# Attention and token mixing in one kernel: the two heads of a pair normalised together, the first batches' scale by another engine, and a new order

## The chip, the cores and the metric

The kernel runs on one core of a Trainium2 chip. The metric is the device time of one execution in microseconds; the median of several executions counts. An execution is a little longer than the span, which goes from the first to the last instruction of the profile. Engines by their names in the profile: PE is TensorE (PEld its weight loads), DVE VectorE, ACT ScalarE, POOL GpSimd, SP the queue that issues the DMAs.

## The reference

```python
# q, k, v: [8, 8, 576, 64] fp32 (batch, head, position, dim)
scores = scale * q @ k.T - slope[h] * |rel|,  masked to 0 <= rel < 128
attn = softmax(scores)                      # + 1e-9 in the denominator
x = (attn @ v), heads side by side          # [8, 576, 512]
theta = x @ w_theta
zr, zi = x * cos(theta), x * sin(theta)
y = w_tok_r @ zr + w_tok_i @ zi             # over positions
u = x + y
out = u + relu(u @ w_ch)
```

q and k are scaled up by about 6.7 before the kernel sees them. All inputs are fp32.

## The kernel before

The kernel writes its steps into a `Plan`: each step has an engine, a cost, the buffers that it reads and writes, and a function that emits its instructions. `Plan.order` simulates the steps by their costs, sorts them by due times, shifts these by the random draws of the seeds in `NUDGES`, and `Plan.run` emits the steps in the order that comes out. So the order on every queue is fixed by the costs, the dependencies and the seeds. Where the plan leaves TensorE idle, `spin` (L363) puts filler matmuls of `white`, into the free columns of the banks of the attention outputs (L367).

Work goes batch by batch, 32 pairs of heads in all, four pairs to a batch. `scores` (L608) does a pair: TensorE's products into `s_ps` (L621), VectorE's bias and minimum (L631), ScalarE's exponential (L635). The first seven pairs (`EARLY`) are transposed on TensorE (L677), copied by ScalarE (L679) and multiplied with v in fp32 (L687). For later pairs the weights are split in two fp16 halves (L644, L646), transposed by a DMA (L649) and multiplied with v split likewise (L601, L603, L705). Head 2p writes into bank `a_psa`, head 2p+1 into `a_psb`. `finish` (L655) then does three VectorE steps for each head: the denominator (L660), its reciprocal (L663) and the normalisation of 320 columns into `x_sb` (L664).

When a batch's eight heads stand, `turn` makes theta and z: x split and transposed by DMA (L811, L812, L816; for batch 0 also by TensorE, L826), theta (L757), range reduction and sine and cosine (L771 to L781), the product with x (L785), z in two fp16 halves (L790, and L411 for the lower half, by VectorE for batches under `QUICK` and by GpSimd for the others). `mix` (L862) and `channels` (L890) are TensorE's large products for the batch before; L868, L872, L875 and L898, L901, L905 are their elementwise steps.

`measure(b)` (L503) finds a power of two by which batch b's v is scaled. For batches under `SUMMED` ScalarE sums |v| over a group of four heads (L516, twice a batch), and VectorE and TensorE turn the sums into one scale (L525 to L545). For the others VectorE takes each head's largest |v| (L521, twice a batch), and L548 to L561 make the scale. What follows (L565 to L568) is common. An early head's `finish` needs that scale's inverse.

The weights come as fp32 and are unpacked on the chip ahead of batch 0's `mix`: `unpack` (L413) loads a chunk (L422) and takes its magnitude (L426 on ScalarE), its low bits (L436 on ScalarE for the first `LOW_C` chunks of `wch`, L440 on VectorE for the others) and puts them together (L432, L443, L452). `halve` splits them in fp16 halves (L478, L481).

Of the kernel before, what the change touches and what calls it, by code (L numbers as in the profile page):

```python
# [25 lines left out]
NT = 5  # L26
# [8 lines left out]
EARLY = 7  # L35
QUICK = 2
# [3 lines left out]
SUMMED = 2  # L40
# [6 lines left out]
LOW_C = 1  # L47
# [5 lines left out]
while RAD * 0.5 > math.pi:  # L53
# [240 lines left out]
def attn_moe_kernel(ctx: ExitStack, tc: tile.TileContext, qt, kt, vx, wth, wtok, wch, band, out):  # L294
# [30 lines left out]
    mx_ring, den_ring = small(2 * NT, 4), small(NT, 4)  # L325
# [35 lines left out]
    a_ring, t_ring, m_ring = banks("a_ps", 2), banks("t_ps", 2), banks("m_ps", 2)  # L361
# [51 lines left out]
    def unpack(src, c, w, held, last, first, summed, magnitude, lowest, raw_buf=None):  # L413
# [8 lines left out]
        issued.append(plan("SP", (0.42, w * 2.55e-3, 2.15), lambda: nc.sync.dma_start(  # L422
# [80 lines left out]
    def measure(b):  # L503
# [6 lines left out]
        for k in range(2):  # L510
            vb = group_v[2 * b + k]
            part = most.tile[:, GROUP * k:GROUP * k + GROUP]
            if b < SUMMED:
# [10 lines left out]
        if b < SUMMED:  # L524
# [71 lines left out]
    def split_values(n):  # L596
        vb, k, (scale, rise, _) = group_v[n // GROUP], n % GROUP, group_scale[n // H]
        buf = v_ring.take()
        vh, vl = buf.tile
        v, vs = vb.tile[:, k, :, :64], scale.tile[:, n % H:n % H + 1]  # L600
        plan("ACT", (0.508, 0.15), lambda: nc.scalar.activation(vh[:, :, :64], v, AF.Copy, scale=vs),  # L601
             r=[(vb, 0), (scale, 0)], w=[(buf, "h")])
        plan("DVE", (0.53, 0.13), lambda: nc.vector.scalar_tensor_tensor(  # L603
            out=vl, in0=v, scalar=vs, in1=vh[:, :, :64], op0=ALU.mult, op1=ALU.subtract),
            r=[(vb, 0), (scale, 0), (buf, "h")], w=[(buf, "l")], port=True)
        return buf, rise.tile[:, n % H:n % H + 1], rise
# [48 lines left out]
    def finish(n, acc, x_buf, vs, read, tiny):  # L655
        h = n % H
        av = acc.tile[:, :NT * 65].rearrange("p (i d) -> p i d", d=65)
        den_buf = den_ring.take()
        den = den_buf.tile[:, :, None]
        plan("DVE", (0.134, 0.13), lambda: nc.vector.tensor_scalar(  # L660
            out=den, in0=av[:, :, 64:65], scalar1=tiny, scalar2=vs, op0=ALU.add, op1=ALU.mult), r=[(acc, 0)] + read,
            w=[(den_buf, 0)])
        plan("DVE", (0.075, 0.13), lambda: nc.vector.reciprocal(out=den, in_=den), w=[(den_buf, 0)])  # L663
        plan("DVE", dve(320), lambda: nc.vector.tensor_tensor(  # L664
            out=x_buf.tile[:, :, h * D:(h + 1) * D], in0=av[:, :, :64], in1=den.broadcast_to([128, NT, D]),
            op=ALU.mult), r=[(acc, 0), (den_buf, 0)], w=[(x_buf, h)])

    def early_head(n, weights, x_buf):
# [22 lines left out]
        finish(n, acc, x_buf, zs.tile[:, 1:2], [(zs, 1)], 1.0e-9)  # L691

    def late_head(n, weights, x_buf):
# [15 lines left out]
        finish(n, acc, x_buf, vs, [(scale, 0)], 1.0e-9 * 2.0 ** PEXP)  # L709
# [259 lines left out]
    for b in range(B):  # L969
        x_buf = x_ring.take()  # L970
        for g in range(PAIRS_OF):
# [5 lines left out]
            for e in range(2):  # L977
                head = early_head if p < EARLY else late_head
                head(2 * p + e, pair_weights[p][e], x_buf)
# [61 lines left out]
```

## Time and profile before

| | |
|---|---|
| median of the runs | 609.73 us (608.84 to 610.28, 3 runs) |
| the profiled execution | 614.84 us |
| its span | 613.0 us |
| instructions in the span | 14313 |

How to read the rows further down: a group of instructions is given by its line, engine and operation, the tile written and the tiles read, the shape, the count, then the busy time in us and the mean of one in ns, then the idle time of the engine just ahead of them with what ended it. A timeline row has the start, the duration, the engine, the line, the tile written and read, and in brackets the idle time ahead of it and its releaser. Neighbours on one engine overlap in these rows, so what an instruction costs a full engine is the distance from its start to the next one's. In a view of the chain, each piece has its start and its length. The granted clock of TensorE is a share of full speed.

### The profile page before, as it was taken

The numbers are of one execution on the slowest core, as the hardware profiler recorded it, in microseconds if no ns is written. First come the engines' busy times: TensorE is split into PE (matmuls) and PEld (weight loads), VectorE is DVE, ScalarE is ACT, GpSimd is POOL, SyncE is SP. The second block draws the span as 40 slices with busy tenths as digits, with TensorE's granted clock in tenths as the row PEclk, the third lists the DMA queues.
The fourth block names the chain that finished last, engine by engine and source line by source line (L and its number), as shares of the span: only waits on it lengthen the run. The fifth ranks groups of instructions, "written<-read, shape, count | busy, mean of one in ns | idle before, by whom it ended". The sixth has DMA issues, their size and how long they took to land.

```text
span 613.0 us, 14313 instructions
## 1 busy us (share of the span) xinstructions
PE 596.3 (97%) x5417; PEld 438.9 (72%) x5417; DVE 531.4 (87%) x1568; ACT 498.8 (81%) x923; POOL 150.4 (25%) x133
## 2 busy tenths in 40 slices
PE   8997999999998999999999999999999999999997
PEld 6786756886676766776677767777677668776775
DVE  5798999999998999899898999999989999658433
ACT  4998999968998889996999689978899699246312
POOL 1000120011240215621474114231232133415100
PEclk9899999999998999999999999999999999999999
DMA  8784762399559892897569775989156734211102
GB/s 313 295 287 148 186 152 57 90 214 183 109 149 218 143 164 68 201 202 165 86 156 226 153 129 120 239 125 209 58 137 143 132 51 108 74 36 39 49 1 78
DMA packets 165541, 87.24 MB, mean 142 GB/s; under 512 B 144736, under 2 KB 153056, under 8 KB 165472
## 3 DMA queue, kind: packets, MB, share of 16 engines
q1 hardware_dynamic: 165472, 86.33, 61.1%
q8 instruction: 42, 0.69, 0.5%
q14 instruction: 27, 0.22, 0.1%
HBM read 41.22 MB, written 9.44 MB: 83 GB/s over the span
## 4 chain that ended last, share of the span: by engine, by line
PE 66%; ACT 18%; DMA 6%; DVE 6%; issue 2%; SPq 1%; POOL 0%; ACTq 0%; DVEq 0%
PE m_psb L862 15%; PE m_psa L862 15%; PE s_ps L621 7%; PE m_psa L890 7%; PE m_psb L890 6%; PE t_psa L757 5%; PE t_psb L757 5%; PE a_psb L705 3%; PE a_psa L705 3%; DMA ptd<-hlb 2%; DMA vbb<-in_vx_dram 2%; ACT sbb L635 2%; ACT sba L635 1%; ACT sbc L635 1%; ACT z_hi L790 1%
## 5 line engine op out<-in xcount | busy, mean ns | idle before, releaser
L862 PEld LDWEIGHTS <-z_hi 128*128 128x128 f16 x1152 | 110.2, 98 | 35.9 <-issue 6.3
L890 PEld LDWEIGHTS <-wch 128*128 128x128 f16 x768 | 73.8, 98 | 24.2 <-issue 4.4
L862 PE MATMUL m_psb<-wtk_hi,z_hi 128*128 128x288 f16 x288 | 82.9, 288 | 0.0
L862 PE MATMUL m_psb<-wtk_hi,z_lo 128*128 128x288 f16 x288 | 82.9, 288 | 0.0
L862 PE MATMUL m_psb<-wtk_lo,z_hi 128*128 128x288 f16 x288 | 82.9, 288 | 0.0
L862 PE MATMUL m_psa<-wtk_hi,z_hi 128*128 128x288 f16 x288 | 82.7, 287 | 0.0
L862 PE MATMUL m_psa<-wtk_lo,z_hi 128*128 128x288 f16 x288 | 82.5, 286 | 0.0
L862 PE MATMUL m_psa<-wtk_hi,z_lo 128*128 128x288 f16 x288 | 82.4, 286 | 0.0
L862 PEld LDWEIGHTS <-z_lo 128*128 128x128 f16 x576 | 56.5, 98 | 14.8 <-DVE z_lo L411 0.3
L411 POOL TENSOR_TENSOR z_lo<-wch_held,z_hi 128x512 f16<-128x512 f32 x28 | 36.8, 1329 | 67.8 <-ACT z_hi L790 67.7
L890 PE MATMUL m_psa<-u,wch 128*128 128x288 f16 x384 | 52.3, 286 | 0.8 <-ACT u_spare L898 0.8
L890 PE MATMUL m_psb<-u,wch 128*128 128x288 f16 x384 | 52.3, 286 | 0.0
L635 ACT ACTIVATE sba<-sba,fixed 128x256 f32<-128x256 f32 (+2 forms) x110 | 44.8, 460 | 3.0 <-DVE fixed L631 2.7
L812 POOL TENSOR_TENSOR hlxa<-x_sba,hlxa 128x512 f16<-128x512 f32 (+1 forms) x12 | 15.4, 1279 | 126.4 <-ACT hlxa L811 126.3
L635 ACT ACTIVATE sbc<-sbc,fixed 128x256 f32<-128x256 f32 (+2 forms) x106 | 43.3, 459 | 3.0 <-DVE fixed L631 2.9
L635 ACT ACTIVATE sbb<-sbb,fixed 128x256 f32<-128x256 f32 (+2 forms) x104 | 42.6, 462 | 3.7 <-DVE fixed L631 3.7
L757 PEld LDWEIGHTS <-xpa 128*128 128x128 f16 x224 | 21.5, 98 | 23.9 <-issue 0.7
L631 DVE CUSTOM_DVE_ANT_0 sba<-s_ps,bands 128x256 f32<-128x256 f32 (+2 forms) x110 | 35.4, 357 | 3.5 <-PE s_ps L621 3.4
L757 PEld LDWEIGHTS <-xpb 128*128 128x128 f16 x224 | 21.3, 98 | 23.5 <-issue 0.7
L631 DVE CUSTOM_DVE_ANT_0 sbc<-s_ps,bands 128x256 f32<-128x256 f32 (+2 forms) x106 | 33.7, 356 | 3.2 <-PE s_ps L621 3.1
L872 ACT ACTIVATE u<-xtfb,fixed 128x288 f16<-128x288 f32 x32 | 16.6, 526 | 24.1 <-DVE xtfb L868 24.1
L631 DVE CUSTOM_DVE_ANT_0 sbb<-s_ps,bands 128x256 f32<-128x256 f32 (+2 forms) x104 | 33.6, 358 | 1.7 <-PE s_ps L621 1.7
(325 smaller groups left out, 1576.9 us busy)
## 6 DMA issues: line engine op xcount, KB each, us to landing
vba<-in_vx_dram SPq DMA_DIRECT2D x6, 780.0 KB, 5.5
out_dram<-xtfa SPq DMA_DIRECT2D x32, 144.0 KB, 2.0
out_dram<-xtfb SPq DMA_DIRECT2D x32, 144.0 KB, 1.8
vbb<-in_vx_dram SPq DMA_DIRECT2D x5, 780.0 KB, 5.6
vbc<-in_vx_dram SPq DMA_DIRECT2D x5, 780.0 KB, 5.6
kra<-in_kt_dram SPq DMA_DIRECT2D x11, 288.0 KB, 4.6
qra<-in_qt_dram SPq DMA_DIRECT2D x11, 288.0 KB, 4.3
qrb<-in_qt_dram SPq DMA_DIRECT2D x11, 288.0 KB, 3.4
```

What stands on the lines that cost most here:

```text
L411: plan(engine, cost, lambda: on.tensor_tensor(out=out, in0=whole, in1=part, op=ALU.subtract), r=r, w=w, port=True)
L621: nc.tensor.matmul(ps.tile[:qn, e, at:at + kn], qr.tile[rows, q0:q0 + qn], kr.tile[rows, k0:k0 + kn], start=True, stop=True)
L631: kn=kn, c0=c0: nc.vector.tensor_tensor_reduce(out=part, in0=source, in1=bands[:qn, (2 * p + e) % H, c0:c0 + kn], scale=-0.125, scalar=3.0 ...
L635: plan("ACT", (0.187 + kn * 0.833e-3, 0.15), lambda part=part, least=least: nc.scalar.activation(part, part, AF.Exp, bias=least, scale=-1. ...
L705: nc.tensor.matmul(av[:, to[0]:to[1], :d], l, r, start=n in STARTS and j == 0, stop=n in STOPS and j == 2)
L757: nc.tensor.matmul(t_ps, a[:, c * 128:c * 128 + 128], w[:, c, :], start=(k == 0 and c == 0), stop=(k == len(prods) - 1 and c == 3))
L790: plan("ACT", (0.52, 0.15), lambda: nc.scalar.copy(z_hi[:, c, :], z), r=key, w=[(z_buf, ("h", c))])
L812: plan("POOL", pool(512), lambda: nc.gpsimd.tensor_tensor(out=lo, in0=x, in1=hi, op=ALU.subtract), r=every + [(hlx, "h")], w=[(hlx, "l")])
L862: nc.tensor.matmul(y.tile[:, :HALF], z[:, c, m * 128:m * 128 + 128], w[:, c, cs], start=(part == 0 and j == 0 and a == 0), stop=(part == 2 ...
L872: plan("ACT", (0.43, 0.15), lambda m=m, cs=cs, at=at: nc.scalar.activation(u_hi[:, m, cs], at, AF.Copy, scale=share), r=[(xtf, ("y", m, hf ...
L890: nc.tensor.matmul(o.tile[:, :HALF], w[:, c, e * 128:e * 128 + 128], u[:, c, cs], start=(k == 0), stop=(k == 11))
```

## The change

The two banks become one tile of two banks, and both heads of a pair end in one `finish`: one denominator step and one reciprocal step over ten columns, then two normalisations as before, one for each head. All of them come behind the second head's product. The ring of denominators holds three pairs where it held four heads.

`SUMMED` is empty: the first two batches' scale comes from VectorE's maximum (L521) like the others'. `QUICK` goes from 2 to 1: the lower half of batch 1's z is made by GpSimd. `LOW_C` goes from 1 to 0: the low bits of the first chunk of `wch` are taken by VectorE. The planned time of the first three weight loads is 0.7 us longer. The seeds are others, and with the costs they give another order of all steps.

```diff
--- before.py
+++ after.py
@@ -33,18 +33,18 @@
 PAIRS = B * H // 2
 PAIRS_OF = H // 2
 EARLY = 7
-QUICK = 2
+QUICK = 1
 TURNED = 0
 TRUE = 3
 MIXED = 1
-SUMMED = 2
+SUMMED = ()
 LIFT = 2.0 ** 16
 ABS_T = 4
 ABS_W = 9
 ABS_C = 4
 LOW_T = 4
 LOW_W = 5
-LOW_C = 1
+LOW_C = 0
 VALUES = ((0, 0), (1, 2))
 
 MAGIC = 1.5 * 2.0 ** 23
@@ -76,12 +76,12 @@
 ROUNDS = 6
 SELF = {"DVE": 0.115, "ACT": 0.13, "POOL": 0.1}
 NUDGES = (
...
 )
 
 
@@ -322,7 +322,7 @@
         assert columns_at[0] <= 320
         return Ring([fixed[:, at + k * width:at + (k + 1) * width] for k in range(count)])
 
-    mx_ring, den_ring = small(2 * NT, 4), small(NT, 4)
+    mx_ring, den_ring = small(2 * NT, 4), small(2 * NT, 3)
     most_ring, whole_ring, spread_ring, scale_ring, rise_ring = (small(H, n) for n in (1, 1, 1, 2, 2))
     zs_ring = small(8, 3)
     white, pale = place("white", [128, 256], BF16), place("pale", [128, 128], BF16)
@@ -358,7 +358,8 @@
     xp_ring = ring("xp", 2, [128, 2, 512], F16)
 
     s_ring = Ring([psum.tile([128, 2, 512], F32, name="s_ps")])
-    a_ring, t_ring, m_ring = banks("a_ps", 2), banks("t_ps", 2), banks("m_ps", 2)
+    pairs_ps = psum.tile([128, 2, 512], F32, name="a_ps")
+    a_ring, t_ring, m_ring = Ring([pairs_ps[:, e] for e in range(2)]), banks("t_ps", 2), banks("m_ps", 2)
 
     def spin(tile, count):
 
@@ -419,7 +420,8 @@
         R, E, M = ((raw_buf, k) for k in "rem")
         ex, low = t[:, 2 * S:2 * S + w], t[:, 3 * S:3 * S + w]
         powers = ex.bitcast(BF16).rearrange("p (n t) -> p n t", t=2)[:, :, 1]
-        issued.append(plan("SP", (0.42, w * 2.55e-3, 2.15), lambda: nc.sync.dma_start(
+        issued.append(plan("SP", (0.42, w * 2.55e-3 + (0.7 if len(issued) < 3 else 0.0), 2.15),
+                           lambda: nc.sync.dma_start(
             out=t[:, :2 * w], in_=src[:, c, :].bitcast(I32)), w=[R]))
         plan.follow(issued[-1], begin)
         if magnitude:
@@ -510,7 +512,7 @@
         for k in range(2):
             vb = group_v[2 * b + k]
             part = most.tile[:, GROUP * k:GROUP * k + GROUP]
-            if b < SUMMED:
+            if b in SUMMED:
                 spare = hl_ring.tiles[k].bitcast(BF16).rearrange("p a b c -> p (a b c)")[:, :GROUP * NT * 64].rearrange(
                     "p (h c d) -> p h c d", h=GROUP, d=64)
                 taken = plan("ACT", (1.26, 0.15), lambda vb=vb, spare=spare, k=k: nc.scalar.activation(
@@ -521,7 +523,7 @@
                 plan("DVE", (1.395, 0.13), lambda vb=vb, part=part: nc.vector.tensor_reduce(
                     out=part, in_=vb.tile[:, :, 1:, :64], axis=mybir.AxisListType.XY, op=ALU.max,
                     apply_absolute_value=True), r=[(vb, 0)], w=[(most, k)])
-        if b < SUMMED:
+        if b in SUMMED:
             plan("DVE", (0.075, 0.13), lambda: nc.vector.tensor_tensor(
                 out=most.tile.rearrange("p (k h) -> p k h", h=GROUP),
                 in0=spread.tile[:, :2, None].broadcast_to([128, 2, GROUP]),
@@ -603,7 +605,8 @@
         plan("DVE", (0.53, 0.13), lambda: nc.vector.scalar_tensor_tensor(
             out=vl, in0=v, scalar=vs, in1=vh[:, :, :64], op0=ALU.mult, op1=ALU.subtract),
             r=[(vb, 0), (scale, 0), (buf, "h")], w=[(buf, "l")], port=True)
-        return buf, rise.tile[:, n % H:n % H + 1], rise
+        first = n % H // 2 * 2
+        return buf, rise.tile[:, first:first + 2, None].broadcast_to([128, 2, NT]), rise
 
     def scores(p, weights):
         late = p >= EARLY
@@ -652,20 +655,24 @@
             for e in range(2):
                 weights[e][group] = pt, ptv[:, e]
 
-    def finish(n, acc, x_buf, vs, read, tiny):
-        h = n % H
-        av = acc.tile[:, :NT * 65].rearrange("p (i d) -> p i d", d=65)
+    def finish(p, accs, x_buf, vs, read, tiny):
+
+        h = 2 * p % H
+        av = pairs_ps[:, :, :NT * 65].rearrange("p e (i d) -> p e i d", d=65)
         den_buf = den_ring.take()
-        den = den_buf.tile[:, :, None]
-        plan("DVE", (0.134, 0.13), lambda: nc.vector.tensor_scalar(
-            out=den, in0=av[:, :, 64:65], scalar1=tiny, scalar2=vs, op0=ALU.add, op1=ALU.mult), r=[(acc, 0)] + read,
+        den = den_buf.tile.rearrange("p (e i) -> p e i", e=2)
+        banks = [(acc, 0) for acc in accs]
+        plan("DVE", (0.15, 0.13), lambda: nc.vector.scalar_tensor_tensor(
+            out=den, in0=av[:, :, :, 64], scalar=tiny, in1=vs, op0=ALU.add, op1=ALU.mult), r=banks + read,
             w=[(den_buf, 0)])
-        plan("DVE", (0.075, 0.13), lambda: nc.vector.reciprocal(out=den, in_=den), w=[(den_buf, 0)])
-        plan("DVE", dve(320), lambda: nc.vector.tensor_tensor(
-            out=x_buf.tile[:, :, h * D:(h + 1) * D], in0=av[:, :, :64], in1=den.broadcast_to([128, NT, D]),
-            op=ALU.mult), r=[(acc, 0), (den_buf, 0)], w=[(x_buf, h)])
-
-    def early_head(n, weights, x_buf):
+        plan("DVE", (0.08, 0.13), lambda: nc.vector.reciprocal(out=den, in_=den), w=[(den_buf, 0)])
+        for e in range(2):
+            plan("DVE", dve(320), lambda e=e: nc.vector.tensor_tensor(
+                out=x_buf.tile[:, :, (h + e) * D:(h + e + 1) * D], in0=av[:, e, :, :64],
+                in1=den[:, e, :, None].broadcast_to([128, NT, D]), op=ALU.mult), r=[(accs[e], 0), (den_buf, 0)],
+                w=[(x_buf, h + e)])
+
+    def early_head(n, weights):
         vb, k = group_v[n // GROUP], n % GROUP
         pt = pt_ring.take()
         for group in range(2):
@@ -688,9 +695,9 @@
                                  start=n in STARTS, stop=n in STOPS)
         plan("PE", pe(1840), multiply, r=[(pt, 0), (pt, 1), (vb, 0)], w=[(acc, 0)])
         zs = group_scale[n // H][2]
-        finish(n, acc, x_buf, zs.tile[:, 1:2], [(zs, 1)], 1.0e-9)
-
-    def late_head(n, weights, x_buf):
+        return acc, zs.tile[:, 1:2, None].broadcast_to([128, 2, NT]), [(zs, 1)], 1.0e-9
+
+    def late_head(n, weights):
         buf, vs, scale = split_values(n)
         acc = a_ring.take()
         av = acc.tile[:, :NT * 65].rearrange("p (i d) -> p i d", d=65)
@@ -706,7 +713,7 @@
                                      stop=n in STOPS and j == 2)
         plan("PE", pe(810), multiply, r=[(buf, "h"), (buf, "l")] + [(weights[g][0], 0) for g in range(2)],
              w=[(acc, 0)])
-        finish(n, acc, x_buf, vs, [(scale, 0)], 1.0e-9 * 2.0 ** PEXP)
+        return acc, vs, [(scale, 0)], 1.0e-9 * 2.0 ** PEXP
 
 
     def turn(b, x_buf, zs):
@@ -974,9 +981,9 @@
                 ready(p)
             if p >= EARLY:
                 ready(p + 1)
-            for e in range(2):
-                head = early_head if p < EARLY else late_head
-                head(2 * p + e, pair_weights[p][e], x_buf)
+            head = early_head if p < EARLY else late_head
+            ends = [head(2 * p + e, pair_weights[p][e]) for e in range(2)]
+            finish(p, [end[0] for end in ends], x_buf, *ends[1][1:])
             pair_weights.pop(p)
         if last is not None:
             mix(*last)
```

## Rows read from the trace of the kernel before

**Rows 1.** The page's first part: busy time, share of the span and number of instructions of each engine.

```profile
PE 596.3 (97%) x5417; PEld 438.9 (72%) x5417; DVE 531.4 (87%) x1568; ACT 498.8 (81%) x923; POOL 150.4 (25%) x133
```

**Rows 2.** Busy time by stage: the stretch and its length, then the busy time of PE, PEld, DVE, ACT and POOL with the number of instructions, the granted clock of TensorE, the DMA engines' busy share and GB/s.

```profile
0.00:20.00 20.00, 16.13 (x129) 13.08 (x130) 8.61 (x45) 10.60 (x20) 1.68 (x15) 0.91 0.90 334
20.00:121.00 101.00, 94.65 (x777) 72.97 (x776) 97.17 (x346) 98.19 (x197) 6.19 (x5) 1.00 0.56 163
121.00:180.00 59.00, 59.00 (x582) 42.95 (x581) 58.18 (x171) 51.34 (x94) 14.12 (x11) 1.00 0.80 165
180.00:200.00 20.00, 18.30 (x175) 13.36 (x173) 17.05 (x70) 17.82 (x34) 1.85 (x2) 0.91 0.85 201
200.00:609.00 409.00, 408.15 (x3763) 296.52 (x3761) 349.92 (x943) 320.37 (x580) 126.58 (x100) 1.00 0.58 122
609.00:613.00 4.00, 0.11 (x1) 0.00 (x0) 0.52 (x1) 0.50 (x1) 0.00 (x0) 1.00 0.21 74
```

**Rows 3.** The same view for line L367, the filler matmuls, alone: PE, PEld, clock, DMA.

```profile
0.00:20.00 20.00, 10.31 (x87) 8.72 (x87) 0.91 0.90 334
20.00:121.00 101.00, 15.38 (x142) 12.02 (x142) 1.00 0.56 163
...
180.00:200.00 20.00, 0.33 (x2) 0.13 (x2) 0.91 0.85 201
```

**Rows 4.** The chain of work that ended last, in order of time, four of its pieces: start, length, engine, tile and line, number of instructions.

```profile
17.41 2.23 PE s_ps L621 x12
...
194.60 2.27 PE m_psb L862 x9
...
253.59 1.22 PE s_ps L621 x12
...
262.11 1.10 PE m_psb L862 x9
```

**Rows 5.** The timeline of ScalarE, VectorE and TensorE at the start, from 13 to 20 us.

```profile
13.50 1.27 ACT L516 ACTIVATE hlb<-vbb 128x1280 bf16<-128x1280 f32 x1 [1.95 <-DMA vbb<-in_vx_dram]
...
16.79 1.26 ACT L516 ACTIVATE hla<-vba 128x1280 bf16<-128x1280 f32 x1
...
18.18 0.17 DVE L525 TENSOR_TENSOR fixed<-fixed 128x8 f32<-128x8 f32 x1 [4.72 <-ACT hla L516]
19.66 0.22 DVE L631 CUSTOM_DVE_ANT_0 sbc<-s_ps,bands 64x64 f32<-64x64 f32 x1 [1.31 <-PE s_ps L621]
...
16.13 1.12 PE L677 MATMUL m_psa<-fixed,sba 128*128 128x128 f32 x4 [2.35 <-ACT pta L679]
```

**Rows 6.** Timeline rows of single instructions that the change drops, adds or moves, with the next start where it is needed: two of `finish`, one L521, one L516 of batch 1, one L436 and one L440.

```profile
25.75 0.21 DVE L660 TENSOR_SCALAR fixed<-a_psa,fixed 128x5 f32<-128x5 f32 x1
25.88 0.75 DVE L452 SCALAR_TENSOR_TENSOR wch_held<-xtfb 128x576 int32<-128x576 int32 x1
26.55 0.18 DVE L663 RECIPROCAL fixed<-fixed 128x5 f32<-128x5 f32 x1
26.65 0.13 DVE L568 TENSOR_TENSOR fixed<-fixed 128x8 f32<-128x8 f32 x1
...
226.83 1.48 DVE L521 TENSOR_REDUCE fixed<-vba 128x4 f32<-128x1280 f32 x1
228.23 0.50 DVE L868 SCALAR_TENSOR_TENSOR xtfb<-m_psa,fixed,xtfb 128x288 f32<-128x288 f32 x1
...
72.72 1.29 ACT L516 ACTIVATE hlb<-vba 128x1280 bf16<-128x1280 f32 x1
...
57.35 0.68 ACT L436 ACTIVATE xtfb<-xtfb 128x512 int32<-128x512 uint16 x1
...
67.62 0.43 DVE L440 TENSOR_SCALAR xtfb<-xtfb 128x512 int32<-128x512 uint32 x1
```

**Rows 7.** VectorE's waits from 0 to 121 us, the one that stands between 50 and 53 us: what waited, for whom, us in total, times, longest.

```profile
DVE u_spare L432 <- ACT u_spare L426: 1.8, 1, 1.8
```

**Rows 8.** The timeline around 190 us: ScalarE, VectorE and TensorE.

```profile
187.63 1.06 ACT L644 ACTIVATE hlb<-sbb 128x1024 f16<-128x1024 f32 x1 [1.61 <-DMA ptd<-hlb]
188.70 1.28 ACT L781 ACT_TABLE_LOAD   x1
...
190.75 1.40 DVE L785 TENSOR_TENSOR fgb<-x_sbb,fgb 64x512 f32<-64x512 f32 x2 [1.72 <-ACT fgb L781]
...
192.90 1.70 PE L621 MATMUL s_ps<-krc,qrc 64*64 64x64 f32 x12 [1.70 <-DVE fixed L631]
```

**Rows 9.** The lower half of z on GpSimd (one line's view: durations in ns, least, median and largest, then first and last start) and on VectorE (groups by line), two groups of L785 of one shape, and two timeline rows at 173 us.

```profile
L411 POOL TENSOR_TENSOR z_lo<-wch_held,z_hi x28: 1150/1350/1934, 226.2 to 572.8; 128x512 f16<-128x512 f32 x28
...
L411 DVE TENSOR_TENSOR z_lo<-wch_held,z_hi 128x512 f16<-128x512 f32 x8 | 5.4, 673 | 0.0
...
L785 DVE TENSOR_TENSOR wch_held<-x_sba,wch_held 64x512 f32<-64x512 f32 x4 | 4.5, 1136 | 0.1
...
L785 DVE TENSOR_TENSOR fga<-x_sba,fga 64x512 f32<-64x512 f32 x4 | 2.7, 680 | 0.8 <-ACT fga L781 0.8
...
173.13 1.27 DVE L785 TENSOR_TENSOR fga<-x_sbb,fga 128x512 f32<-128x512 f32 x1
...
173.04 2.02 POOL L905 TENSOR_TENSOR xtfa<-xtfa,u_spare 128x288 f32<-128x288 f32 x2 [2.12 <-ACT u_spare L898]
```

**Rows 10.** TensorE's waits from 108 to 121 us, one row.

```profile
PE a_psb L687 <- DVE x_sbb L664: 0.8, 1, 0.8
```

**Rows 11.** The queue that issues the DMAs, from 0 to 20 us, one row.

```profile
5.50 0.74 SPq L493 DMA_DIRECT2D krb<-in_kt_dram  x1
```

12 rows, old and new, of the table NUDGES are left out of this document.

## The prediction

> **What bounds the kernel now.** I read the page's busy times first [rows 1]: TensorE is busy 97% of the span, VectorE 87%, ScalarE 81%. But TensorE's busy time holds the filler matmuls of `spin` (L367), which do no work of the reference, so the second view is the busy time by stage [rows 2], and the third the same stages for L367 alone [rows 3]. From them the time in which TensorE does nothing useful can be written down. From 0 to 20 us: 20 - (16.13 - 10.31) = 14.2 us. From 20 to 121 us: 101 - (94.65 - 15.38) = 21.7 us. From 121 to 180 us: none. From 180 to 200 us: 1.7 us idle and 0.3 us of filler, and a granted clock of 0.91, which is 9% of 20 us = 1.8 us more; 3.8 us in all. From 200 to 609 us: 0.85 us. Then 3.9 us of tail behind the last matmul. So there are two regimes. Behind 121 us TensorE is the bound: what another engine saves there gives time back only out of 3.8 + 0.85 us. Ahead of 121 us TensorE waits to be fed, and VectorE and ScalarE are both full: 97.2 and 98.2 us of the 101 us from 20 to 121 [rows 2].
>
> Who feeds it late? The timeline from 13 to 20 us [rows 5] shows what ScalarE's sum over v (L516) costs there. ScalarE waits 1.95 us for `vbb`, and L516 then holds it twice, 1.27 and 1.26 us. VectorE stands 4.72 us in front of L525, which waits for L516, and another 1.31 us for scores. TensorE waits 2.35 us for ScalarE's copy L679, which stands behind L516, and then takes 2.23 us for twelve scores that it does in 1.22 us later [rows 4].
>
> The profiled execution took 614.84 us, its span 613.0 us; the median of the runs is 609.73 us, 0.8% under it. The sum is made on the profile and carried to the median as a difference.
>
> **The change, part by part.** One denominator and one reciprocal step for a pair. What counts on a full engine is the distance from one start to the next: L660 takes 0.13 us (25.75 to 25.88), L663 takes 0.10 us (26.55 to 26.65) [rows 6], though their listed durations are 0.21 and 0.18. Each pair drops one of each: 0.23 us, 32 pairs 7.4 us. No row shows the new step, with two banks and ten columns; I bound it by one L660 and by two of them (0.13 to 0.26), and take 0.15: L521 does 1280 columns in 1.40 us, so five more columns are next to nothing. At the upper end the pair saves 0.10 us instead of 0.23. Some 6 pairs end ahead of 121 us: 1.4 us off VectorE there. The 6 us behind that lie beside a full TensorE and are worth nothing unless they take away a stall.
>
> The first two batches' maximum goes to VectorE. ScalarE loses four L516, 1.27 us each (the third stands at 72.72 us [rows 6]). VectorE gains four L521 of 1.40 us (226.83 to 228.23 [rows 6]). The small steps behind it change from five to four on VectorE: one of L663's kind less for each batch, which I count as 0.15 us. Batch 0's two reductions can run where VectorE now stands idle (13.5 to 19.7 us, 6.0 us of waits against 2.8 us of work). Batch 1's two, at 72 to 81 us, fall into full time: +2.8 us. What then stands behind the waiting reduction on VectorE is what stood behind L525: the scores' bias and minimum (L631) and the unpacking of the weights. The wait for `vbb` moves with it from ScalarE to VectorE. The unpacking of the last weight (`LOW_C`) takes 0.68 us from ScalarE (L436) and gives VectorE 0.43 us (L440) [rows 6].
>
> So ahead of 121 us ScalarE is relieved by 1.95 + 2.53 us at the very start and 2.53 + 0.68 us later: 7.7 us. VectorE gets 2.8 + 0.43 - 1.4 - 0.3 = +1.5 us in the full stretch, and is 6.0 - 2.8 = 3.2 us earlier into it if the waits go: net 1.7 us earlier. The later of the two decides, so I take VectorE's 1.7 us. One end is ScalarE's: up to 6 us (7.7 less what the loads hold back: the DMA engines were at 0.90 of their time in the first 20 us [rows 2]). The other end is +4.3 us: nothing of the idle time is used (2.8) and the 1.5 stands. VectorE's longest wait in the rest of this part, 1.8 us [rows 7], is for ScalarE's L426, which a freer ScalarE may shorten.
>
> `QUICK`: batch 1's nine z_lo differences move from VectorE to GpSimd. VectorE loses 9 x 0.61 = 5.5 us (0.67 listed [rows 9], less the 0.07 by which neighbours overlap, as for L660); GpSimd gets 9 x 1.35 = 12 us [rows 9], beside 1.85 us of the 20 in which batch 1's mix begins [rows 2]. VectorE pays part of it back. L785 takes 0.68 us in one group of four and 1.14 us in another of the same shape, and one took 1.27 us just as GpSimd ran L905 (from 173.04) [rows 9]. I take 0.2 us for each GpSimd step, 2 us; net -3.5 us of VectorE from 150 to 200 us. The worst row (1.27 less 0.68) gives 9 x 0.6 = 5.4 us, which eats the gain. Each z_lo also comes 0.68 us later to TensorE; the last ones ahead of the mix at 194.60 us [rows 4] are those that could be late.
>
> This is what the Trainium skill says under "SBUF — State Buffer", section "Who interferes with whom": a VectorE instruction with two SBUF inputs and a GpSimd instruction that reads SBUF exclude each other for the whole instruction. L785's 1.27 us against 0.68 agrees. By that rule alone each GpSimd step could hold VectorE for all of its 1.15 us or more, 10 us for nine, and the move would cost VectorE 5 us net instead of saving 3.5; this is the third rival. The same section says that VectorE's tensor_reduce doesn't contend; the reductions that the change adds would then not be slowed.
>
> The stall at 180 to 200 us: ScalarE waits 1.61 us for a transposing DMA, loads a table at 188.70 [rows 8]; VectorE waits 1.72 us for the sine, the scores wait for VectorE's L631, TensorE stands 1.70 us and then takes 2.27 us for nine matmuls that take 1.10 later [rows 4]: half its speed, the lower of its two levels (1.2 against 2.4 GHz). The change takes 3.5 us of VectorE's work from this stretch and gives a new order, but neither the DMA nor the table goes. I take half of the 3.8 us: -1.9. Ends: 0 and -3.8.
>
> The banks: head A's normalisation now waits for head B's product, so A's bank is held longer, and the next pair's first product may wait for the pair's two short steps and A's normalisation. A wait of that kind is there once ahead of 121 us, 0.8 us for L664 [rows 10]. Behind 121 us 25 pairs share 489 us, some 19 us each, so nothing there; ahead of it TensorE isn't the bound, so I cost it at nothing too. Without that cover it is 0.8 us for each of 6 pairs, 4.8 us.
>
> Sum: 1.7 + 1.9 = 3.6 us less: span 609.4 us, the execution 611.2 us, the median 606.1.
>
> **The rivals.** A: nothing that can be measured. VectorE's relief lies beside TensorE, the start's order is held by the loads (`krb` is issued at 5.50 us [rows 11], behind both loads of v, and its scores start at 17.41 [rows 4]), and the stall stays: 609.7. For it speaks that the loads fill the first 20 us; against, that VectorE and ScalarE both stand idle in front of L516.
> B: slower, VectorE as the bound of the start. It is at 96% there, and 5.6 + 0.43 us come to it; if the two early reductions delay the scores instead of filling the 4.72 us, TensorE's full stretch begins at 125 us: 609.7 + 4.3 = 614.0. It decides if VectorE has no wait left between 13.5 and 20 us and yet TensorE's full stretch begins later.
> C: GpSimd's nine steps each hold VectorE to their end: 9 x 1.15 = 10 us (the shortest L411 takes 1.15 [rows 9]) against the 5.5 saved, 4.9 us more for VectorE ahead of batch 1's mix. Half of it reaches TensorE, 2.5 us, while the start gains 1.7: 610.5. L785's 1.27 us speaks for it, the groups at 0.68 against.
> D: the start gains all of ScalarE's 6 us and the stall goes: 609.7 - 9.8 = 599.9.
> E: the change doesn't do what it says, because the order, made anew, puts a stall like the one at 191 us elsewhere or the banks hold TensorE: +3.8 - 1.7, 611.8.
>
> **How the numbers follow.** Forecast 0.47, A 0.19, B 0.15, C 0.05, D 0.09, E 0.05. 0.2% is 1.2 us, about what a measurement of this kernel tells from no change. The forecast and D are faster; A, most of C and a sliver of the forecast are the same; B and E are slower: 0.55, 0.24, 0.21. The forecast's own range is 602.0 (the start halfway to ScalarE's end, -3.9, and the whole stall, -3.8) to 608.5. With the other cases, leaving out half of D and the far half of B, it is 600.5 to 613.
>
> **What would show it.** L516 gone and L521 sixteen times, two of them at 13 to 19 us in place of VectorE's wait; ScalarE with some 6 us less busy time ahead of 121 us; 32 steps each at the denominators and reciprocals; the start of TensorE's full stretch one to three us earlier; the granted clock at 1.00 through the stretch in which batch 1's mix begins. I am wrong if TensorE's useless time ahead of its full stretch is not smaller, or if new idle time or a lower clock stands behind 200 us.

## The result, and the profile after

The changed kernel takes 616.34 us (median of 9 runs, 613.84 to 617.39), the kernel before in the same comparison 611.41 us (9 runs, 608.84 to 613.62): 0.8% slower, ratio 1.008 with a 95% interval of 1.0056 to 1.0103. The forecast was 606.1 us, 3.6 us below the median that the prediction had for the kernel before; the result lies outside the range, on the other side. The profiled execution took 616.34 us, the same as the median. In three of the later runs (b_max, b_free, b_one_free) one execution each was in a slower state and is left out of the ratio.

First the head of the changed kernel's page, then its busy times by stage (the stretch and its length, the engines' busy times with the number of instructions, the granted clock, DMA share, GB/s), then two of the stages for the fillers alone (now L368). They answer to [rows 1 to 3].

```profile
span 614.5 us, 14271 instructions
PE 594.8 (97%) x5418; PEld 438.2 (71%) x5418; DVE 531.6 (87%) x1498; ACT 498.4 (81%) x916; POOL 165.8 (27%) x142
```

```profile
core 0: us, PE busy (x) PEld busy (x) DVE busy (x) ACT busy (x) POOL busy (x), PEclk, DMA share, GB/s
0.00:20.00 20.00, 17.52 (x156) 14.79 (x156) 13.79 (x59) 11.59 (x24) 1.69 (x15) 1.00 0.90 337
20.00:121.00 101.00, 90.05 (x728) 69.53 (x729) 91.63 (x318) 90.76 (x180) 6.44 (x5) 0.98 0.54 158
...
180.00:200.00 20.00, 19.67 (x198) 14.84 (x197) 18.87 (x54) 19.75 (x42) 11.42 (x10) 1.00 0.76 199
```

```profile
0.00:20.00 20.00, 10.42 (x90) 9.02 (x90) 1.00 0.90 337
20.00:121.00 101.00, 14.00 (x143) 11.86 (x143) 0.98 0.54 158
```

The page's totals tell nothing: 97, 87 and 81% as before. The stages do. ScalarE is relieved as foretold and VectorE works earlier in the first 20 us. But from 20 to 121 us all three engines are *less* busy than before, VectorE by 5.5 us, ScalarE by 7.4, TensorE by 4.6 [rows 2]. Of ScalarE's 7.4 us some 3.2 are work that was taken from it there; VectorE was given work there and yet is less busy, so something makes it wait. The waits of TensorE, then of VectorE, in that stretch (waiting line, releaser: total us, times, longest), four of TensorE's and three of VectorE's:

```profile
PE a_ps L368 <- DVE x_sba L670: 4.2, 4, 2.0
PE s_ps L624 <- DVE fixed L634: 1.6, 3, 0.8
...
PE a_ps L368 <- DVE fixed L665: 0.6, 1, 0.6
PE a_ps L694 <- DVE x_sbb L670: 0.6, 1, 0.6
```

```profile
DVE x_sba L670 <- PE a_ps L694: 2.5, 1, 2.5
DVE x_sba L670 <- PE a_ps L368: 2.0, 2, 1.5
...
DVE x_sbb L670 <- PE a_ps L694: 1.1, 1, 1.1
```

L670 is the normalisation (L664 before), L694 the early heads' product (L687). TensorE stands 5.4 us behind VectorE's normalisations and denominators, 4.8 us of it in front of fillers, which do no work; and VectorE stands 5.6 us in front of normalisations until a product or a filler is done. In the kernel before, TensorE stands once for a normalisation there, 0.8 us [rows 10], and VectorE has no wait of 0.2 us or more for TensorE. One of these places in the timeline (start, duration, engine, line, tiles; in brackets the idle time ahead and its releaser):

```profile
26.67 0.48 DVE L670 TENSOR_TENSOR x_sba<-a_ps,fixed 128x320 f32<-128x320 f32 x1
...
27.20 0.56 PE L368 MATMUL a_ps<-white 128*128 128x187 bf16 x5 [0.75 <-DVE x_sba L670]
...
28.04 1.90 PE L694 MATMUL a_ps<-vba,ptc 128*128 128x130 f32 x16
...
29.98 0.49 DVE L670 TENSOR_TENSOR x_sba<-a_ps,fixed 128x320 f32<-128x320 f32 x1 [2.49 <-PE a_ps L694]
30.10 0.46 ACT L638 ACTIVATE sbb<-sbb,fixed 128x192 f32<-128x192 f32 x1
```

Read it from the top. VectorE normalises head A. A filler waits for that. Then comes the next pair's product of head A, into the first bank. VectorE's second normalisation reads head B, the *second* bank, which this product does not write, and still it stands 2.49 us until the product is done. What is queued behind it on VectorE (the unpacking of the weights at 30.39 us) waits as well.

### The profile page after: what moved, and what is told of

Its sections match the earlier page's. It is cut to its first block, busy times and chain, and to the rows that moved or that the text cites. A ratio compares the mean times of both kernels' runs of the same rounds, so it can differ in the third digit from the quotient of the medians.

```text
span 614.5 us, 14271 instructions
## 1 busy us (share of the span) xinstructions
PE 594.8 (97%) x5418; PEld 438.2 (71%) x5418; DVE 531.6 (87%) x1498; ACT 498.4 (81%) x916; POOL 165.8 (27%) x142
## 4 chain that ended last, share of the span: by engine, by line
PE 70%; DVE 14%; ACT 10%; DMA 4%; issue 2%; SPq 0%; ACTq 0%; DVEq 0%
PE m_psa L869 17%; PE m_psb L869 16%; PE s_ps L624 7%; PE t_psa L764 6%; PE t_psb L764 6%; PE a_ps L712 6%; PE m_psa L897 6%; PE m_psb L897 5%; DMA vbb<-in_vx_dram 1%; DMA u_spare<-in_wtok_dram 1%; ACT sba L638 1%; DVE fixed L523 1%; DMA xtfb<-in_wch_dram 1%; DVE sbb L634 1%; DVE sbc L634 1%
## 5 line engine op out<-in xcount | busy, mean ns | idle before, releaser
L412 POOL TENSOR_TENSOR z_lo<-wch_held,z_hi 128x512 f16<-128x512 f32 x32 | 43.5, 1376 | 49.2 <-ACT z_hi L797 43.1
L819 POOL TENSOR_TENSOR hlxb<-x_sbb,hlxb 128x512 f16<-128x512 f32 (+1 forms) x12 | 16.5, 1376 | 71.9 <-ACT hlxb L818 70.4
```

What stands on the lines that cost most here:

```text
L412: plan(engine, cost, lambda: on.tensor_tensor(out=out, in0=whole, in1=part, op=ALU.subtract), r=r, w=w, port=True)
L819: plan("POOL", pool(512), lambda: nc.gpsimd.tensor_tensor(out=lo, in0=x, in1=hi, op=ALU.subtract), r=every + [(hlx, "h")], w=[(hlx, "l")])
```

## The experiments

The theory from these rows: the merged `a_ps` is one tile, and the program's semaphores guard whole tiles. So a product into one bank, or a filler, and a normalisation of the other bank wait for each other (theory 1). The rivals: the new order loses the time, whatever the tiles (theory 2), and VectorE, which got the reductions, is the bound of the start (theory 3, the prediction's second rival). Names with a_ are made from the changed kernel and keep its order of steps, names with b_ from the kernel before and keep its own; so no run mixes an edit with another order. All ratios are to the kernel before, run on the same chip; they are not the quotients of two medians, from which they differ by up to 0.2%.

| run | median us | ratio to before | 95% interval |
|---|---|---|---|
| changed kernel | 616.34 | 1.0080 | 1.0056 to 1.0103 |
| a_two_tiles | 610.15 | 0.9968 | 0.9950 to 0.9986 |
| a_two_free | 614.07 | 1.0027 | 1.0003 to 1.0052 |
| a_free_fill (one tile) | 614.78 | 1.0056 | 1.0030 to 1.0082 |
| a_two_back | 609.62 | 0.9972 | 0.9949 to 0.9994 |
| a_two_z | 610.77 | 0.9992 | 0.9972 to 1.0012 |
| a_two_sum | 612.19 | 1.0005 | 0.9986 to 1.0025 |
| b_same | 611.54 | 0.9987 | 0.9966 to 1.0008 |
| b_one_tile | 616.78 | 1.0082 | 1.0052 to 1.0112 |
| b_max | 613.30 | 1.0029 | 1.0008 to 1.0050 |
| b_z | 608.83 | 0.9974 | 0.9953 to 0.9995 |
| b_free | 612.73 | 1.0027 | 1.0005 to 1.0049 |
| b_one_free (one tile) | 619.52 | 1.0126 | 1.0086 to 1.0166 |

**Two tiles again (a_two_tiles).** The pair still ends at once and the order is kept; each bank is a tile, so the denominators take two steps.

```diff
-    pairs_ps = psum.tile([128, 2, 512], F32, name="a_ps")
-    a_ring, t_ring, m_ring = Ring([pairs_ps[:, e] for e in range(2)]), banks("t_ps", 2), banks("m_ps", 2)
+    a_ring, t_ring, m_ring = banks("a_ps", 2), banks("t_ps", 2), banks("m_ps", 2)
...
+            for e in range(2):
+                nc.vector.scalar_tensor_tensor(out=den[:, e], in0=avs[e][:, :, 64], scalar=tiny, in1=vs[:, e],
+                                               op0=ALU.add, op1=ALU.mult)
```

> The changed kernel in its own order, but the two banks are two tiles again (the pair's denominators are then two steps of five columns in the place of one of ten). Theory 1 (the merged end makes TensorE and VectorE wait for each other: with one tile, head B's normalisation stands behind the next pair's product into the other bank, 2.5 + 1.1 us in the profile after, and fillers stand behind normalisations, 4.8 us): the first of the two goes, the fillers stay as they are, so 2 to 4 us less than the changed kernel's 616.3, about 613. Theory 2 (the new order loses the time, whatever the tiles): 616.3 or up to 1 us more for the 32 steps added. Theory 3 (VectorE is the bound of the start, by the reductions that it got): 616.3 plus up to 1 us as well.

Measured: 610.15 us, 6.2 less than the changed kernel, more than expected; the intervals of the two ratios lie far apart. The whole loss is gone, and 0.3% is gained. The same place in its timeline (L671 is the normalisation, L695 the product, L367 the filler):

```profile
26.10 0.57 PE L367 MATMUL a_psb<-white 128*128 128x187 bf16 x5
...
26.70 0.48 DVE L671 TENSOR_TENSOR x_sba<-a_psa,fixed 128x320 f32<-128x320 f32 x1
...
27.24 2.00 PE L695 MATMUL a_psa<-vba,ptc 128*128 128x130 f32 x16
...
27.45 0.48 DVE L671 TENSOR_TENSOR x_sba<-a_psb,fixed 128x320 f32<-128x320 f32 x1
```

The filler no longer waits, and head B is normalised at 27.45 us *beside* the product into the other bank. VectorE's unpacking begins at 27.85 us in place of 30.39. From 20 to 121 us VectorE's only wait for TensorE is one of 0.2 us for scores. Theories 2 and 3 expected 616 or more and fall as the cause of the loss.

**One tile alone, in the kernel before (b_one_tile).** The same two lines the other way round, and nothing else: per-head ends, old order.

> The kernel before in its own order with its own per-head end, and only the two banks made one tile. Theory 1 in its narrow form (the tile alone makes the waits): ten normalisations wait for TensorE where three did, so 1 to 3 us more than the kernel before, 612.5 to 614.5. Theory 2, theory 3, and theory 1 in its wide form (it takes the later, merged end as well, which leaves banks with readers while TensorE idles): within 0.5 us of the kernel before.

Measured: 616.78 us, 0.8% slower than before, more than the 1 to 3 us that were expected. One allocation makes a loss as large as that of the whole change; the wide form of theory 1, which asked for the merged end too, is wrong. Its timeline from 112 us (L688 is the product, L665 the normalisation), then a later stage of it:

```profile
112.50 0.49 DVE L665 TENSOR_TENSOR x_sbb<-a_ps,fixed 128x320 f32<-128x320 f32 x1
...
113.05 0.56 PE L368 MATMUL a_ps<-white 128*128 128x187 bf16 x5 [1.23 <-DVE x_sbb L665]
113.45 1.93 PE L688 MATMUL a_ps<-vbc,ptd 128*128 128x130 f32 x16
115.41 0.49 DVE L665 TENSOR_TENSOR x_sbb<-a_ps,fixed 128x320 f32<-128x320 f32 x1 [1.75 <-PE a_ps L688]
...
115.96 2.00 PE L688 MATMUL a_ps<-vbc,ptc 128*128 128x130 f32 x16 [0.58 <-DVE x_sbb L665]
...
119.50 3.25 PE L688 MATMUL a_ps<-vba,ptb 128*128 128x130 f32 x16 [1.54 <-DVE x_sbb L665]
```

```profile
110.00:121.00 11.00, 7.61 (x60) 6.84 (x60) 7.25 (x22) 9.57 (x22) 0.00 (x0) 0.95 0.44 84
121.00:130.00 9.00, 9.00 (x55) 7.10 (x55) 7.00 (x24) 3.58 (x6) 0.00 (x0) 0.68 0.45 105
```

The normalisation at 115.41 us is of the other head than the product ahead of it, and waits for it; the product behind it waits for the normalisation: the two engines go in turns. And behind it the granted clock is 0.68 for 9 us, a mix of its two levels (1.2 and 2.4 GHz), just behind a stretch in which TensorE was busy 7.61 of 11 us; the last product takes 3.25 us for what the one ahead of it does in 2.00. So in this order the waits cost twice. Over its runs the mean clock is 0.994 here and 0.997 in the kernel before; in the changed kernel's runs it is 0.998, the same as in a_two_tiles, so no such second loss shows there.

**The kernel before once more (b_same).**

> The kernel before once more, unchanged. Its first profiled execution took 614.84 us where the median of its runs is 611.4. If the first profile is an untypical execution, then this one is 2 to 4 us shorter and the difference has a place: the stall of TensorE at 180 to 200 us (3.8 us) is the first suspect, the start up to 121 us the second. If it is typical, this profile shows 614 to 615 us with the stall in it, and profiled executions are longer than others by 3 us.

Measured: 611.54 us. The profiled execution took 609.03 us, the shortest of the twelve runs, 5.8 us less than the first one, where 2 to 4 were expected; its span is 607.3 us where the first profile had 613.0. Two stages of it, all work:

```profile
0.00:20.00 20.00, 17.53 (x151) 14.30 (x151) 11.38 (x61) 12.93 (x26) 1.68 (x15) 1.00 0.90 337
...
180.00:200.00 20.00, 18.64 (x188) 13.99 (x185) 18.29 (x68) 18.75 (x38) 2.11 (x3) 1.00 0.77 186
```

In both stages the first profile showed a clock of 0.91 [rows 2]; here it is 1.00. Two dips of 9% of 20 us would be 3.6 us, and 1.7 us less idle in these two stages most of the rest, if each dip cost its full share. That is not shown: b_z, further down, has the same 0.91 in the first 20 us and the shortest span of all, 606.7 us. In the first profile that clock fell to 0.57 from 16 to 20 us, behind four us in which TensorE was busy 1.78; here TensorE was busy 3.06 of the same four and the clock stayed at 1.00. The stall at 180 to 200 us is there in both, but it costs 1.7 us (1.36 idle, 0.3 of fillers), not 3.8. The profile on which the prediction rests was of an execution 3.4 us longer than the median of the nine runs.

**Fillers into free banks only.** `run` takes a bank for fillers only if its next use in the order is a product: with two tiles for that bank (a_two_free, 92 fillers of 236; b_free, 97 of 231), with one tile for both banks (a_free_fill, 90; b_one_free, 92). In a_two_back the old rule stays where no bank is free (206). The edit with two tiles (with one tile, both `False` are `True`):

```diff
-                k = min(range(len(tiles)), key=lambda k: used[k])
-                spin(tiles[k], int(FILL * (s.start - max(last, used[k])) / SPIN))
+                free = [k for k, u in enumerate(users) if not u or u[0].engine == "PE"]
+                if False and len(free) < len(tiles):
+                    free = []
+                if free:
+                    k = min(free, key=lambda k: used[k])
+                    since = max(used) if False else used[k]
+                    spin(tiles[k], int(FILL * (s.start - max(last, since)) / SPIN))
```

> As the one with two tiles, and a filler goes only into a bank whose next use in the order is a product, never into one that a step still has to read. 92 fillers are left of 236. Theory 1: no normalisation waits for a filler any more and hardly a filler for a normalisation; the rest of the lost time comes back, 611 to 612, unless the granted clock falls without the fillers, which the profile would show. Theory 2 and theory 3: 616.3 or more.

> The changed kernel with its one tile and in its own order; a filler only when the next use of both banks in the order is a product (90 fillers). It differs from the kernel with two tiles and free banks (92 fillers, 614.07 us, clock 0.90 from 20 to 121 us) in the tile alone, at nearly the same fillers. If the fillers carry what the one tile costs (theory 1a): 613 to 615 us, as that one. If the products and normalisations of different banks carry it, since four normalisations still stand behind the other bank's product (theory 1b): 3 us or more above it, 617 to 620.

> The changed kernel with two tiles, and a filler goes first into a bank whose next use is a product; only where there is none, by the old rule (206 fillers of 236, 2 normalisations behind TensorE in the place of 6). If the fillers' waits on their own bank still cost something (theory 1a): 1 to 2 us less than the 610.15 of two tiles alone. If not, or if the 30 fillers less take the clock down in places (rival): 610 to 612.

> The kernel before with its two tiles and in its own order; a filler only goes into a bank whose next use in the order is a product (97 fillers of 231), so no normalisation waits for TensorE any more. It is the base for the next run. If the fillers are worth what they were in the new order (92 in the place of 236 cost 0.6%, by a lower granted clock from 60 to 100 us): 613 to 615 us.

> The same with one tile, and a filler only when the next use of both banks is a product (92 fillers). Here seven normalisations still wait for TensorE, all of them for the other head's product. If waits between products and normalisations of different banks carry the cost of one tile in this order (theory 1b): about 5 us above the base, as with all fillers. If the fillers carry it (theory 1a, as the new order showed it: 0.3% with few fillers against 1.1% with all): within 2 us of the base.

Measured: with two tiles and few fillers 614.07 us; the fillers left out cost 0.6%. The stage from 20 to 121 us of that kernel:

```profile
20.00:121.00 101.00, 87.83 (x610) 64.49 (x608) 94.80 (x326) 93.56 (x182) 6.38 (x5) 0.90 0.56 162
```

The clock there is 0.90 where the changed kernel with two tiles and all fillers has 0.98. The expectation of 611 to 612 was wrong by just the condition that it named. In the old order the fillers left out cost 0.3% (b_free), less than expected. Its profile shows a clock of 1.00 from 20 to 121 us and 0.94 ahead of it; over the runs of its ratio the mean clock is 0.995 against 0.998 in the kernel before, so the loss goes with the clock there too, if less clearly.

What then does one tile cost at few fillers? In the old order 1.0126 against 1.0027, 1.0%, as much as with all fillers: so fillers are not needed for the loss, and products and normalisations of different heads are what is left to carry it (theory 1b). A lower clock goes with it: 0.990 in the mean over the runs of its ratio, against 0.995 in b_free's. The one trace of b_one_free is of an execution of 624.57 us, well above its median, and can't split the two. In the new order 1.0056 against 1.0027, 0.3% with an interval from nothing to 0.7%, where all fillers made it 1.1% (1.0080 against 0.9968): there a good part hangs on the fillers, as the 4.8 us of waits in front of them say. How large that part is stays open: both kernels with few fillers also run at a lower clock, which may hide waits. a_two_back gives 0.9972, the same as a_two_tiles: waits of a filler in its own bank cost nothing that shows, unless the 30 fillers less cost what the waits gave back (its clock is 0.97 from 20 to 121 us, against 0.98).

**Batch 1's lower halves (`QUICK`).** a_two_z puts the nine differences back on VectorE in the new order, b_z gives them to GpSimd in the old one; only the engine that issues them is another.

> The changed kernel with two tiles in the order of before this run, but batch 1's nine z_lo differences are done by VectorE again. By the prediction's step on QUICK (GpSimd spares VectorE 3.5 us net, part of which reaches TensorE at 150 to 200 us): 0.5 to 2 us more than 610.15. By its third rival (GpSimd's steps hold VectorE to their end): 1 to 2.5 us less. If that stretch is TensorE's whatever VectorE does: within 0.5 us.

> The kernel before in its own order, but batch 1's nine z_lo differences are done by GpSimd. By the run that put them back on VectorE in the new order (0.24% slower than with GpSimd): about 1.5 us less than the kernel before. By the prediction's step on QUICK: 0 to 2 us less, out of the stall at 180 to 200 us, which has 1.4 us of idle in the second profile of before. If GpSimd's steps hold VectorE (third rival), or z_lo comes late to TensorE: 1 to 2.5 us more.

Measured: a_two_z is 0.24% above a_two_tiles, with an interval from nothing to 0.5%, and b_z 0.26% below the kernel before (0.05 to 0.47%). The two agree in size. Where b_z gains, its stage from 180 to 200 us shows (with its first 20 us ahead of it); the last row is the same stage of a_two_z:

```profile
0.00:20.00 20.00, 16.26 (x135) 13.39 (x136) 9.42 (x50) 11.19 (x22) 1.69 (x15) 0.91 0.91 337
...
180.00:200.00 20.00, 19.93 (x201) 14.97 (x200) 19.79 (x69) 19.94 (x40) 6.88 (x7) 1.00 0.79 178
```

```profile
180.00:200.00 20.00, 20.00 (x199) 15.38 (x198) 19.49 (x61) 18.99 (x43) 5.07 (x5) 1.00 0.86 186
```

TensorE's idle time there goes from 1.36 us (b_same) to 0.07. The edit takes the stall away, 1.3 us of idle time. In the new order the gain must lie elsewhere: a_two_z has TensorE busy 20.00 of these 20 us, with VectorE doing the differences, so the stall was gone without `QUICK` there, and where a_two_z loses its 0.24% is not shown.

**The scale from the maximum.** b_max lets VectorE take the maximum where ScalarE summed, in the old order; a_two_sum lets ScalarE sum (into a scratch tile) where VectorE took the maximum, in the new one.

```diff
-                taken = plan("ACT", (1.26, 0.15), lambda vb=vb, spare=spare, k=k: nc.scalar.activation(
-                    spare, vb.tile[:, :, 1:, :64], AF.Abs, accum_out=spread.tile[:, k:k + 1]), r=[(vb, 0)],
+                taken = plan("ACT", (1.26, 0.15), lambda vb=vb, k=k: nc.vector.tensor_reduce(
+                    out=spread.tile[:, k:k + 1], in_=vb.tile[:, :, 1:, :64], axis=mybir.AxisListType.XYZ, op=ALU.max,
+                    apply_absolute_value=True), r=[(vb, 0)],
```

> The kernel before in its own order, but VectorE takes the largest |v| of a group where ScalarE summed |v| (four times, two of them in the first 20 us, two at 72 to 81 us); the small steps behind it stay. By the prediction's step on the start (VectorE stood idle in front of L525 anyway): 0 to 2 us less than the kernel before's 611.6. By the second rival (VectorE is the bound of the start and gets 4 x 1.4 us): 2 to 4 us more.

> The changed kernel with two tiles in its own order, but for the first two batches ScalarE sums |v| over a group (into a scratch tile of its own) at the places in the order where VectorE took the maximum; the small steps behind it are as many as there. If VectorE as the bound of the start is what made the maximum cost 1.8 us in the order of before (second rival): 1 to 2 us less than the 610.15 of two tiles, about 608.5. If the new order, made for the maximum, has already taken that cost away: 610 to 613, the sums then stand in front of ScalarE's exponentials.

Measured: the maximum costs 0.3% in the old order, 1.8 us, a little under the 2 to 4 us of the second rival; and the sum costs 0.4% against a_two_tiles in the new one. In each order, giving the step to the engine for which the order was not made loses. So theory 3 shows its cost in the old order and none in the new one; no run changes this step alone together with an order made for it, so what it gives or costs there by itself stays open.

## Why the prediction was wrong

**The banks: this is the step that failed.** The prediction costed them "at nothing" and named 4.8 us "without that cover". The runs measured 5.1 us (b_one_tile, 616.78 against 611.66 of the kernel before in that comparison) and 6.2 us (the changed kernel against a_two_tiles). The size without cover was about right, but by luck: the cover was not there, and the mechanism was another one. The prediction looked at how long a bank is held by the pair's later end. With two tiles that later end is still there, and costs nothing that shows (a_two_tiles). What costs is that two banks became one thing to wait for, which stands in the diff as one allocation, and which the prediction passed over. And the argument "ahead of it TensorE isn't the bound" forgot that such waits go both ways: VectorE, busy 97.2 of 101 us there [rows 2], waited 5.6 us for TensorE.

TensorE's useless time ahead of 121 us, idle plus fillers, worked out as in the prediction, shows the same. The stages of b_same (its first 20 us stand above), a_two_tiles and b_one_tile:

```profile
20.00:121.00 101.00, 95.71 (x786) 73.88 (x783) 98.09 (x344) 99.29 (x198) 6.19 (x5) 1.00 0.60 171
```

```profile
0.00:20.00 20.00, 17.84 (x157) 15.27 (x158) 13.68 (x59) 11.64 (x24) 1.69 (x15) 1.00 0.91 339
20.00:121.00 101.00, 94.85 (x776) 74.48 (x776) 97.11 (x342) 95.23 (x187) 6.14 (x5) 0.98 0.60 169
```

```profile
0.00:20.00 20.00, 15.67 (x145) 12.84 (x147) 10.78 (x59) 12.15 (x25) 1.69 (x15) 1.00 0.91 341
20.00:121.00 101.00, 92.09 (x751) 71.19 (x752) 93.83 (x329) 97.82 (x196) 6.35 (x5) 1.00 0.56 165
```

The fillers in these stages are 10.92 and 14.64 us in b_same, 10.42 and 15.03 in a_two_tiles, 10.08 and 14.63 in b_one_tile. So the useless time is 33.3 us in the kernel before (b_same: 13.39 up to 20 us and 19.93 behind it; 35.9 in the prediction's profile) and 33.8 in a_two_tiles (12.58 + 21.18), but 37.9 in the changed kernel (12.90 + 24.95) and 38.0 in b_one_tile (14.41 + 23.54). The prediction's own sign of being wrong, that this time is not smaller, came true. Carried on to 200 us, the sum nearly closes for b_one_tile: 3.7 us more useless time than in b_same (38.7 and 35.0) and 3.0 us of clock (0.95 from 121 to 180 us), against a span that is 7.4 us longer. For the changed kernel it closes only in part: a_two_tiles pays some of it later, with 2.9 us idle from 121 to 180 us where the changed kernel has 0.4, so up to 200 us the two differ by 1.8 us (39.0 and 37.2), and their spans by 3.8. That the one tile makes the loss is shown by the times; where in the trace all of it lies is not.

On banks the Trainium skill ("PSUM — Partial Sum Buffer", section "PSUM bank collisions raise a hardware error") says that two engines in one bank collide, in other columns of it too, if they are in the same group of 32 partitions, while accesses to different banks run clean; its section "Summary: rules for kernel authors" says to guard by bank. No run here shows a collision. The second half the trace bears out: in a_two_tiles normalisation and product ran side by side in two banks.

**The stall at 180 to 200 us: right in the order of before, in cause and nearly in size.** -1.9 us were taken; b_z measured -0.26%, 1.6 us (0.3 to 2.9), and shows the idle time gone. But 1.8 of the "3.8 us" was a dip of the clock that the second profile does not have. The third rival did not come: nine GpSimd steps more made the kernel faster, not 5 us slower on VectorE.

By the rule of the Trainium skill that the prediction named there ("SBUF — State Buffer", section "Who interferes with whom") VectorE could have lost 10 us; b_z shows no such loss in the time. Its trace shows VectorE held beside three of GpSimd's steps (L412; L411 before):

```profile
155.73 2.50 POOL L412 TENSOR_TENSOR z_lo<-wch_held,z_hi 128x512 f16<-128x512 f32 x2
157.05 1.50 DVE L876 SCALAR_TENSOR_TENSOR u<-xtfa,fixed,u 128x288 f16<-128x288 f32 x1
...
181.55 2.45 POOL L412 TENSOR_TENSOR z_lo<-fga,z_hi 128x512 f16<-128x512 f32 x2
181.59 1.39 DVE L777 TENSOR_SCALAR fgb<-fgb 64x512 int32<-64x512 int32 x1
...
189.10 1.15 POOL L412 TENSOR_TENSOR z_lo<-fgb,z_hi 128x512 f16<-128x512 f32 x1 [5.10 <-ACT z_hi L791]
189.41 0.87 DVE L581 SCALAR_TENSOR_TENSOR fixed<-fixed 128x1 f32<-128x1 f32 x1
```

In b_same the same three steps take 0.50, 0.70 and 0.15 us: 2.4 us held in all, near the 2 us that the prediction took. L785, for which it took them, did not meet these steps of GpSimd and takes the same time in both kernels.

**The start: its parts came, its sum did not.** The maximum of v stands at 9.68 us, the 4.72 us wait in front of L525 [rows 5] is gone, ScalarE is busy 6.4 us less ahead of 121 us (11.59 + 90.76 against 10.60 + 98.19), of which 5.8 us is work that was taken from it. -1.7 us were taken for it. a_two_tiles, which holds it all without the one tile, gains 0.32% in all, of which `QUICK` is 0.24% by a_two_z. So for the start, the merged end and the new order together some 0.1% remains, which is not told from nothing. TensorE's useless time says the same: 33.8 against 33.3 us.

**The rivals.** The fifth rival said "the banks hold TensorE" and had the sign, with a chance of 0.05 and 611.8 us for a result that is 4.9 us above before. The second rival (614.0 us, VectorE as the bound of the start) comes near in number, but its mechanism explains only what b_max shows, and not the loss: a_two_tiles has the same reductions. The sign that was to decide it, VectorE without a wait from 13.5 to 20 us and more useless time of TensorE, is there in the changed kernel; but VectorE has no wait there in a_two_tiles either, so the sign did not decide.

**The new steps** cost less than was taken for them. From one start to the next, as the prediction counted, the denominator step over two banks (L665, 32 of them) takes 0.08 us at the median, where 0.15 was taken, and the reciprocal over ten columns 0.13 where one over five took 0.10. So this term was not what failed.

The better version is a_two_tiles, or b_z, which is the kernel before with batch 1's differences on GpSimd alone: both 0.3% faster than before, and not to be told apart.

## What to carry to other kernels

When a diff makes one tile out of two, ask who touches the halves at once, and count the waits on both sides: here one allocation cost 0.8 to 1.1%, and what the merged steps saved could not be told from nothing. A wait that costs the idle engine nothing may still hold the bound engine on its other end. And look at a second profile of the kernel before, where one can be had, if its profiled execution lies above the median: a clock of 0.91 in a stage may come in one execution and not in the next.

## What was not expected of the hardware

Two profiled executions of the same kernel had spans of 613.0 and 607.3 us, with a granted clock of 0.91 or of 1.00 in the same two stages. Some 140 fillers of 0.1 us each, which compute nothing, were worth 0.6% of the time in one order and 0.3% in the other.
